# Fused attention, MoE and gated convolution on one core: small tiles allocated first, so that every large tile starts at a multiple of 256 bytes

## The chip, the cores and the metric

The kernel runs on one core of one Trainium2 chip. Its time is the device time of one launch in microseconds (us), the median of three timed runs. Five engines work side by side, each in its own program order and tied to the others by semaphores: PE (matmul, with its weight loads shown as PEld), DVE, ACT and POOL, and SP, which issues the transfers (DMA). SBUF is the memory on the chip from which the engines read: 128 partitions, in which a tile takes the same range of bytes in each. "Address" here is the byte in the partition at which a tile starts, and "remainder" that address modulo 256.

## What is computed

Three blocks in a row, all in float32, cut here to what matters:

```python
def _attn_ref(x, state):                 # x [8, 8, 512, 64], state [8, 8, 32, 64]
    a  = softmax(x @ state.T * scale)    # tokens read the state
    xread = a @ state
    a2 = softmax(state @ x.T * scale)    # the state reads the tokens
    sread = a2 @ x
    return concat([xread, sread], axis=2)          # [8, 8, 544, 64]

def _moe_ref(x, g_ln, w_ch1, w_ch2):               # x [8, 544, 512]
    xn = (x - mean) / sqrt(var + 1e-06) * g_ln
    return x + maximum(xn @ w_ch1, 0.0) @ w_ch2    # 512 -> 2048 -> 512

def _moe2_ref(x, w_in, conv_w, w_out):             # 512 -> 1024 -> 512
    h = maximum(x @ w_in, 0.0)
    gate = sigmoid(conv over 3 neighbours of h)
    return h * gate @ w_out
```

## The kernel before, in words

The work goes by batches of 512 tokens; the 32 state rows of all eight batches are gathered into one tail of 256 columns. The first block's hidden layer is made by `L1` (16 slices of the 2,048 hidden columns) and consumed at once by `L2`, which accumulates into the four banks `acc`. For batches 1 to 7 the weights of `L1` are folded with the state (`z_tiles`, Z tiles ZH and ZL), and the attention of the next batch (`attn`) and the norm of this one (`lnorm`) are woven in between the slices. Batch 0 runs in a hand-written order (`START`) together with the loading and conversion of the weights. After that the second block goes over (batch, slice) pairs: `L3` makes a slice, `conv`, `gate_1` and `gate_2` convolve and gate it on ACT, DVE and POOL, and `L4` multiplies it three steps later.

A float32 product is made from three passes of a faster type: each operand is split into a high and a low half (tiles with H and L in their names, or the two halves of one tile), and `three` (lines 623 to 626) issues high by high, high by low and low by high. In `T.matmul(o, s, m)` the second argument is the stationary operand, which PE loads as weights, and the third is the moving one, which streams through with up to 512 columns. The rows of the profile name the moving tile first: `acc<-ZH,w` has ZH moving over w.

All SBUF tiles come from one pool with one buffer per tag. A tag gets its place when it is first asked for, behind the tags asked for before it, padded to a multiple of 32 bytes; a later tile of the same tag takes the same place. `new` (line 68) asks by tag. Large tiles have sizes in multiples of 512 bytes, so only the small ones shift what comes behind them. The first tile starts at byte 16,512, remainder 128. Adding up the sizes in the order of first use gives the remainders of the kernel before:

| remainder | large tiles |
|---|---|
| 128 | hH, hL, XTt, s_in, s_raw, s_H, s_L, ident, ones |
| 160 | gmean (behind gcol) |
| 64 | XT0, XT1, r0 to r5, w2_0 to w2_8, w2_10, w2_11, bP, bU, AH0, AL0, sbd0, ctmp0, ctmp1 (behind eps, hmask and cw) |
| 128 | bR (behind ms0) |
| 192 | r6 (behind ms1) |
| 0 | w2_14 (behind m20 and z20) |
| 64 | w2_e, ZH0, ZL0, bV, rs0, tn, bQ (behind m21 and z21) |
| 96 | w2_13 (behind rm0) |
| 128 | w2_9, ZH1, ZL1, AH1, AL1, sbd1 (behind rm1) |
| 192 | w2_12, w2_15, rs1, v0, v1 (behind m10) |

The weights of the second block are put into places that have become free (`homes`, line 928): slices of `w_in` into AH0, AL0, r1 to r5 and XTt, slices of `w_out` into r0, r6, v0, v1, ZH0, ZL0, ZH1 and ZL1. The gated slices, stationary in `L4`, take w2_14, w2_15 and w2_3 in turn (`gm`, line 1023); the tail's gated slices take w2_2. The input of the second block, moving in `L3`, lies in XT0 and tn for even batches and in XT1, AH1 and AL1 for odd ones.

Of the kernel before, what the change touches and what calls it, by code (L numbers as in the profile page):

```python
# [9 lines left out]
F32 = mybir.dt.float32  # L10
# [7 lines left out]
P = 128  # L18
# [5 lines left out]
KC = DM // P  # L24
M1 = 16
FF = 8
# [16 lines left out]
def kernel(  # L43
# [18 lines left out]
    sb = ctx.enter_context(tc.tile_pool(name="sb", bufs=1))  # L62
# [5 lines left out]
    def new(tag, shape, dt=F32):  # L68
        count[0] += 1
        return sb.tile([P, *shape], dt, tag=tag, name=f"{tag}_{count[0]}")  # L70

    count = [0]

    hid = {c: new(f"h{c}", [2, S], F32 if c == "H" else F32R) for c in "HL"}
    XT = {}
# [7 lines left out]
    gcol = new("gcol", [KC])  # L83
    gmean = new("gmean", [KC, P])
    eps = new("eps", [1])
    hmask = new("hmask", [2, 2])
    cw = new("cw", [3 * FF])
# [17 lines left out]
    def flat(ap):  # L105
        return ap.rearrange("p a c -> p (a c)")
# [248 lines left out]
    def token_weights_3(aT, b, g, c):  # L355
        h, l = (t[:, g, c] for t in parts[b])
        A.activation(h, aT, AF.Copy)
        V.tensor_tensor(l, aT, f32(h), op=ALU.subtract)
# [67 lines left out]
    def tokens_start(h, xT, B):  # L426

        W = 256
        for g in range(2):
            xp = B["xp"][g].rearrange("p (q ck c) -> p q ck c", q=2, ck=2)  # L430
            for ck in range(2):
                for ql in range(2):
                    q = 2 * g + ql
                    T.transpose(xp[:, ql, ck], x0[:, 2 * h + ck, 2 * q : 2 * q + 2], ident)
            dst = xT[:, 2 * g : 2 * g + 2].rearrange("p q (ck c) -> p q ck c", ck=2)
            A.activation(dst, xp, AF.Copy)
        yield
        sc = B["sc"].rearrange("p (ck q m) -> p ck q m", ck=2, q=KC)
        for q in range(KC):
            for ck in range(2):  # L440
                T.matmul(
                    sc[:, ck, q], xT[:, q, P * ck : P * ck + P], sbd[0][:, q], start=True, stop=True
                )
        sT = new(B["U"], [16, NS])
        m1 = sb.tile([P, 16], F32, name=f"ms{h}")
        sc = B["sc"].rearrange("p (a n) -> p a n", n=NS)
        wide = m1.unsqueeze(2).to_broadcast([P, 16, NS])
        V.tensor_reduce(m1, sc, axis=AX.X, op=ALU.max)
        V.tensor_tensor(sT, sc, wide, op=ALU.subtract)
        A.activation(sT, sT, AF.Exp, scale=0.125)  # L450
        yield
        V.tensor_reduce(m1, sT, axis=AX.X, op=ALU.add)
        V.tensor_scalar(m1, m1, EPS_SM, None, op0=ALU.add)
        V.reciprocal(m1, m1)
        V.tensor_tensor(sT, sT, wide, op=ALU.mult)
        yield
        aT = B["aT"].rearrange("p (g ck c) -> p g ck c", g=2, ck=2)
        a4 = flat(sT).rearrange("p (ck g m) -> p ck g m", ck=2, g=2)
        for g in range(2):
            for ck in range(2):  # L460
                T.transpose(aT[:, g, ck], a4[:, ck, g], ident)
        aT = B["aT"].rearrange("p (g c) -> p g c", g=2)
        token_weights_3(aT, 0, slice(0, 2), HALF[h])
# [403 lines left out]
    def warm_steps():  # L867
# [5 lines left out]
    streams = {  # L873
        "s": (state_start(), acc),
        "0": (tokens_start(0, x0T[0], sets[0]), acc),
        "1": (tokens_start(1, x0T[1], sets[1]), acc),
        "a": (firsts(), acc),
        "b": (seconds(), acc),
# [77 lines left out]
    for u, follow in zip(units, [*units[1:], None]):  # L956
        n = S if u < NB else TAIL
# [132 lines left out]
    n = len(steps)  # L1090
    for i in range(n + 3):
        if i == FF + 3:
            tc_start.close()
        if i < n:
            b, f = steps[i]
# [14 lines left out]
        if i >= 3:  # L1110
            j = i - 3
            b, f = steps[j]
# [44 lines left out]
```

## Time and profile before

| | us |
|---|---|
| three timed runs | 1163.63, 1166.12, 1167.33 |
| their median | 1166.12 |
| span of the profiled execution | 1163.6 |
| PE busy in it | 1128.9 (97%) |
| PE weight loads | 845.3 (73%) |
| DVE busy | 720.9 (62%) |
| ACT busy | 442.2 (38%) |
| POOL busy | 182.3 (16%) |

The profile is one execution, from its first instruction to its last; the page gives no time around it. Busy times of PE come from modelled ends of pipelined matmuls, so a busy PE is not PE at its peak: two matmuls overlap in the list, and their distance is read from their starts.

### The profile page before, as it was taken

What the parts mean: (1) busy time and instruction counts of PE and PEld (TensorE: products, weight loads), DVE (VectorE), ACT (ScalarE), POOL (GpSimd) and SP (SyncE); (2) the same over time, 40 slices, a digit from 0 to 9 for tenths busy, and PEclk for the clock granted to TensorE, in tenths of its full rate; (3) what the DMA queues carried; (4) which work ended last, traced back from release to release, by engine and by line L of the source; (5) the groups of instructions that cost most, each with busy time, mean ns of one, the idle gap of its engine ahead of it and who ended that gap; (6) DMA issues with size and microseconds to landing.
All of it is one profiled execution on the core that took longest, in us unless ns stands there. A gap on an engine that the chain in (4) does not pass through costs nothing. (4 is left out here: it accounts for less than half of the span.)

```text
span 1163.6 us, 14521 instructions
## 1 busy us (share of the span) xinstructions
PE 1128.9 (97%) x5393; PEld 845.3 (73%) x5393; DVE 720.9 (62%) x1134; ACT 442.2 (38%) x788; POOL 182.3 (16%) x298
## 2 busy tenths in 40 slices
PE   6999999999999999999999999999999999999997
PEld 4544467777777777777667797788788888888885
DVE  5888567565574665664765723577676666666563
ACT  4655334332232233233233312555353444334332
POOL 2433200000000000000000000365342212222110
PEclk7999999999999999999999999999999999999999
DMA  8565262332334224323332125221112102100001
GB/s 281 159 201 163 71 234 84 83 118 72 76 111 111 73 94 109 95 84 79 96 83 82 73 73 199 95 84 58 37 55 73 37 37 83 37 37 37 1 37 45
DMA packets 129282, 106.29 MB, mean 91 GB/s; under 512 B 103332, under 2 KB 107452, under 8 KB 128188
## 3 DMA queue, kind: packets, MB, share of 16 engines
q1 hardware_dynamic: 129212, 105.37, 29.2%
q8 instruction: 42, 0.69, 0.2%
q14 instruction: 28, 0.23, 0.1%
HBM read 83.85 MB, written 21.50 MB: 91 GB/s over the span
## 5 line engine op out<-in xcount | busy, mean ns | idle before, releaser
L644 DVE SCALAR_TENSOR_TENSOR hL<-ph,hH 128x512 fp32r<-128x512 f32 (+1 forms) x128 | 83.4, 655 | 172.9 <-ACT hH L643 172.5
L624 PE MATMUL acc<-hH,w 128*128 128x512 f32 (+1 forms) x480 | 189.0, 394 | 0.0
L625 PE MATMUL acc<-hL,w 128*128 128x512 f32 (+1 forms) x480 | 181.8, 379 | 0.0
L626 PE MATMUL acc<-hH,w 128*128 128x512 f32 (+1 forms) x480 | 181.8, 379 | 0.0
L643 ACT ACTIVATE hH<-ph 128x512 fp32r<-128x512 f32 (+1 forms) x128 | 72.7, 568 | 196.3 <-PE ph L626 158.9
L1070 DVE SCALAR_TENSOR_TENSOR w<-w,cw,w 128x544 f32<-128x544 f32 x128 | 109.8, 859 | 35.2 <-POOL w L1068 33.3
L624 PEld LDWEIGHTS acc<-hH,w 128*128 128x128 f32 x480 | 90.3, 188 | 44.7 <-issue 15.6
L624 PE MATMUL ph<-AH,ZH 128*128 128x512 f32 x256 | 106.6, 416 | 1.6 <-ACT ZH L599 1.6
L626 PEld LDWEIGHTS acc<-hH,w 128*128 128x128 f32 x480 | 90.2, 188 | 18.2
L625 PEld LDWEIGHTS acc<-hL,w 128*128 128x128 f32 x480 | 90.3, 188 | 16.7 <-DVE hL L644 0.3
L626 PE MATMUL ph<-AH,ZL 128*128 128x512 f32 x256 | 101.4, 396 | 0.0
L625 PE MATMUL ph<-AL,ZH 128*128 128x512 f32 x256 | 100.8, 394 | 0.0
L212 POOL TENSOR_TENSOR ctmp<-ctmp,AH 128x512 int32<-128x512 int32 x1 | 1.3, 1311 | 589.5 <-DVE ctmp L211 589.5
L1051 ACT ACTIVATE w<-w 128x544 f32<-128x544 f32 x64 | 42.1, 658 | 135.2 <-DVE w L1070 135.2
L1058 DVE TENSOR_TENSOR w<-w,w 128x512 fp32r<-128x512 f32 x64 | 50.0, 782 | 43.7 <-ACT w L1057 43.0
L1052 DVE TENSOR_TENSOR w<-w,w 128x544 f32<-128x544 f32 x64 | 48.6, 760 | 40.0 <-ACT w L1051 40.0
L624 PEld LDWEIGHTS ph<-AH,ZH 128*128 128x128 f32 x256 | 48.2, 188 | 22.9 <-issue 8.8
L1057 ACT ACTIVATE w<-w 128x512 fp32r<-128x512 f32 x64 | 40.4, 631 | 52.4 <-DVE w L1052 50.3
L626 PEld LDWEIGHTS ph<-AH,ZL 128*128 128x128 f32 x256 | 48.2, 188 | 12.9 <-DVE ZL L600 2.0
L1068 POOL TENSOR_SCALAR w<-w,cw 128x544 f32<-128x544 f32 x64 | 47.9, 749 | 54.4 <-ACT w L1064 51.2
L625 PEld LDWEIGHTS ph<-AL,ZH 128*128 128x128 f32 x256 | 48.3, 189 | 10.2 <-issue 1.2
L667 PE MATMUL acc<-hH,w 128*128 128x512 f32 x112 | 50.4, 594 | 0.0
(465 smaller groups left out, 2257.5 us busy)
## 6 DMA issues: line engine op xcount, KB each, us to landing
r<-w1d SPq DMA_DIRECT2D x64, 512.0 KB, 5.2
r<-in_moe_w_ch_dram SPq DMA_DIRECT2D x16, 512.0 KB, 5.0
w<-in_moe_w_ch_dram SPq DMA_DIRECT2D x16, 512.0 KB, 8.2
x2d<-XT SPq DMA_DIRECT2D x8, 1024.0 KB, 4.9
bP<-in_x_dram SPq DMA_DIRECT2D x112, 64.0 KB, 2.3
bP<-in_x_dram SPq DMA_DIRECT2D x28, 256.0 KB, 3.7
out_dram<-w SPq DMA_DIRECT2D x24, 256.0 KB, 2.1
w1d<-r SPq DMA_DIRECT2D x8, 512.0 KB, 5.3
```

The lines of the kernel that those rows point to most:

```text
L624: T.matmul(o, lh, rh, start=first, stop=False)
L625: T.matmul(o, lh, rl, start=False, stop=False)
L626: T.matmul(o, ll, rh, start=False, stop=last)
L643: A.activation(h, p, AF.Relu)
L644: V.scalar_tensor_tensor(l, p, 0.0, f32(h), op0=ALU.max, op1=ALU.subtract)
L667: T.matmul(acc[d], whole2[m][:, c], h, start=m == 0, stop=m == M1 - 1)
L1051: A.activation(c, c, AF.Sigmoid)
L1052: V.tensor_tensor(c, c, h[:, 1 : SEQ + 1], op=ALU.mult)
L1057: A.activation(g[:, 0], c[:, :S], AF.Copy)
L1058: V.tensor_tensor(g[:, 1], c[:, :S], f32(g[:, 0]), op=ALU.subtract)
L1068: G.tensor_scalar(c, h[:, 0:SEQ], cw[:, f : f + 1], 0.0, op0=ALU.mult, op1=ALU.add)
L1070: V.scalar_tensor_tensor(c, h[:, k : k + SEQ], cw[:, k * FF + f : k * FF + f + 1], c, op0=ALU.mult, op1=ALU.add,)
```

## The change

Ahead of the first large tile, one tile is asked for under each of the small tags (m20, z20, m21, z21, eps, rm0, rm1, m10, gcol, hmask, cw), so that these tags have their places at the front. The two tiles ms0 and ms1, which were made where they are used, are made there too and kept in a list. A filler of 64 bytes, `pad`, follows. With it the small tiles take 640 bytes, from 16,512 to 17,152, which is 67 times 256, and each large tile behind starts at remainder 0. The tiles of the tags are asked for again later as before; those first ones are never written or read.

```diff
     count = [0]
 
+    for tag, n in (
+        *((t, 1) for t in ("m20", "z20", "m21", "z21", "eps")),
+        *((t, 2) for t in ("rm0", "rm1")),
+        ("m10", 16), ("gcol", KC), ("hmask", 4), ("cw", 3 * FF),
+    ):
+        sb.tile([P, n], F32, tag=tag, name=f"{tag}_0")
+    ms = [sb.tile([P, 16], F32, name=f"ms{h}") for h in range(2)]
+    sb.tile([P, 16], F32, name="pad")
+
     hid = {c: new(f"h{c}", [2, S], F32 if c == "H" else F32R) for c in "HL"}
...
         sT = new(B["U"], [16, NS])
-        m1 = sb.tile([P, 16], F32, name=f"ms{h}")
+        m1 = ms[h]
         sc = B["sc"].rearrange("p (a n) -> p a n", n=NS)
```

The change moves no instruction: on every engine the built programs have the same instructions in the same order with the same waits, and differ in addresses, line numbers (9 more) and the numbers in tiles' names. So at the place in the second block where `L4` of one slice ends, the tail's product follows and `L3` of a later slice begins, PE's row stands before as

```order
L624 MATMUL acc3_80<-ZH0_622_5740,w2_15_614_5610 128x512
L625 MATMUL acc3_80<-ZH0_622_5740,w2_15_614_5610 128x512
L626 MATMUL acc3_80<-ZH0_622_5740,w2_15_614_5610 128x512
L624 MATMUL pat1_84<-ZH0_622_5740,w2_2_612_5608 128x512
L625 MATMUL pat1_84<-ZH0_622_5740,w2_2_612_5608 128x512
L626 MATMUL pat1_84<-ZH0_622_5740,w2_2_612_5608 128x512
L624 MATMUL pat0_83<-XT0_642_6697,AH0_566_5271 128x512
L625 MATMUL pat0_83<-tn_643_6698,AH0_566_5271 128x512
```

and after it the same rows stand at the same place: only the remainders of the tiles change, here from 64 and 192 to 0.

## Rows read from the trace of the kernel before

**Rows 1.** The head of the page: span, busy time and instructions of each engine.

```profile
span 1163.6 us, 14521 instructions
PE 1128.9 (97%) x5393; PEld 845.3 (73%) x5393; DVE 720.9 (62%) x1134; ACT 442.2 (38%) x788; POOL 182.3 (16%) x298
```

**Rows 2.** Stretches: length; PE, PEld, DVE, ACT, POOL busy (instructions); granted clock; DMA; GB/s.

```profile
0.00:150.00 150.00, 134.16 (x520) 71.98 (x520) 109.99 (x183) 75.55 (x134) 46.48 (x60) 0.95 0.58 181
150.00:660.00 510.00, 502.60 (x2575) 369.14 (x2574) 311.88 (x545) 168.19 (x296) 0.00 (x0) 1.00 0.33 95
660.00:774.00 114.00, 113.30 (x619) 94.75 (x618) 50.22 (x80) 42.59 (x79) 23.05 (x17) 1.00 0.33 116
774.00:819.00 45.00, 42.14 (x223) 35.46 (x221) 35.37 (x45) 23.28 (x43) 26.35 (x33) 1.00 0.17 59
819.00:1155.00 336.00, 336.00 (x1462) 273.76 (x1463) 212.66 (x282) 131.94 (x236) 86.44 (x190) 1.00 0.12 41
870.00:1150.00 280.00, 280.00 (x1215) 227.97 (x1214) 176.81 (x235) 109.11 (x195) 69.09 (x155) 1.00 0.11 39
```

**Rows 3.** PE in order of time, from 961.83 us: start, length, instruction.

```profile
961.83 0.40 PE L624 MATMUL pat<-ZH,w 128*128 128x512 f32 x1
962.07 0.39 PE L625 MATMUL pat<-ZH,w 128*128 128x512 f32 x1
962.30 0.40 PE L626 MATMUL pat<-ZH,w 128*128 128x512 f32 x1
962.53 0.39 PE L624 MATMUL pat<-XT,AH 128*128 128x512 f32 x1
962.76 0.39 PE L625 MATMUL pat<-tn,AH 128*128 128x512 f32 x1
962.99 0.39 PE L626 MATMUL pat<-XT,AH 128*128 128x512 f32 x1
...
971.15 0.39 PE L626 MATMUL ph<-XT,AL 128*128 128x512 f32 x1
```

**Rows 4.** PE in order of time, from 922.89 us.

```profile
922.89 0.39 PE L624 MATMUL acc<-ZH,w 128*128 128x512 f32 x1
923.12 0.40 PE L625 MATMUL acc<-ZH,w 128*128 128x512 f32 x1
923.35 0.39 PE L626 MATMUL acc<-ZH,w 128*128 128x512 f32 x1
923.58 0.40 PE L624 MATMUL acc<-ZH,w 128*128 128x512 f32 x1
...
925.22 0.39 PE L625 MATMUL acc<-ZH,w 128*128 128x512 f32 x1
```

**Rows 5.** PE in order of time, from 787.79 us.

```profile
787.79 0.50 PE L624 MATMUL ph<-XT,r 128*128 128x512 f32 x1
788.13 0.40 PE L625 MATMUL ph<-tn,r 128*128 128x512 f32 x1
...
789.28 0.39 PE L624 MATMUL ph<-XT,r 128*128 128x512 f32 x1
...
790.41 0.39 PE L626 MATMUL ph<-XT,r 128*128 128x512 f32 x1
```

**Rows 6.** PE's waits: who waited for whom, us in total, times, longest.

```profile
PE pat L485 <- ACT bQ L478: 4.1, 3, 3.1
...
PE ph L624 <- ACT w L1064: 2.8, 2, 1.5
...
PE acc L434 <- DMA XT<-in_x_dram: 1.4, 2, 0.9
...
PE ph L416 <- DMA s_raw<-in_state_dram: 0.6, 1, 0.6
```

**Rows 7.** DVE's line 600: shortest, median and longest in ns.

```profile
L600 DVE TENSOR_TENSOR ZL<-pat,ZH x64: 677/681/693, 36.6 to 743.4; 128x512 fp32r<-128x512 f32 x64
```

## The prediction, made before the changed kernel was run

> **What bounds the kernel now.** I read the head of the page first: the matrix engine is busy 1,128.9 of 1,163.6 us, DVE 62%, ACT 38%, POOL 16% [rows 1]. Then the table by stages: from 819 to 1,155 us PE is busy 336.00 of 336.00 us, from 150 to 660 us 502.60 of 510, and the granted clock there is 1.00, the upper of its two levels (2.4 GHz) [rows 2]. So after the first 150 us the time is a row of matmuls, and what matters is how far apart two matmuls start. A busy time does not tell that: a row of the list in order of time shows 0.39 us for one 512-column matmul while the next starts 0.23 us later [rows 3]. The spacing comes from the starts. Between 870 and 1,150 us there are 1,215 matmuls, all of 512 columns, without a gap; a row that lasts 0.39 us is counted if its end reaches into the stretch, so they stand for 280.39 us, and 280.39 / 1,215 is 230.8 ns each [rows 2].
>
> Then I asked whether the spacing depends on where the operands lie, since that is all that the change moves. It does. The stretch from 961.83 us has 41 matmuls whose moving tiles (ZH0, XT0, tn, ZL0) and stationary tiles (w2_2, AH0, w2_3, AL0) all lie at remainder 64 of 256. Its first four spacings are 0.24, 0.23, 0.23, 0.23 us; from 962.76 to 971.15 us there are 37 spacings in 8.39 us, 226.7 ns each, and it ends when the next pair brings another remainder [rows 3]. The block from 922.89 us has ZH1 (remainder 128) moving over w2_15 (192): from 922.89 to 925.22 us ten spacings in 2.33 us, 233 ns each [rows 4]. I sorted the spacings after 150 us by remainder: where all tiles of a matmul, of the ten before it and of the next shared one remainder, 64, 128 or 192, each of the 164 spacings was 226 or 227 ns, whatever multiple of 256 bytes lay between the tiles; where remainders mixed, they lay between 225 and 241. So what counts in these rows is that the remainders agree, not which one it is.
>
> **The change, part by part.** It adds no instruction, takes none away and moves none: on each engine the same instructions stand in the same order with the same waits, and the early tiles of a tag are never written. What changes is the address of nearly every tile, and after it every large tile has remainder 0.
>
> Matmuls: the three products of each pair of halves (lines 624 to 626) are 3,696 matmuls with 512 columns: 7 x 16 x (6 + 12) = 2,016 in the seven batches of the first block after batch 0, 96 in batch 0, 64 x 12 = 768 in the first product of the second block, and 64 x 12 + 48 = 816 in its last. Of these 3,464 are followed within 250 ns by another of the kind, by their starts in the list in order of time; the others stand before a gap or another shape. At 230.7 to 230.8 ns before and 226.7 ns after, each gives back 4.0 ns, together 13.9 us. That is the upper bound.
>
> Against it stands that a row of matmuls needs time to settle. After a break (another shape or a wait) the spacing is irregular even where all remainders agree: after the break at 787.79 us the five spacings from 788.13 to 789.28 us take 1.15 us, 230 ns each, and the next five, to 790.41 us, 1.13 us, 226 ns each [rows 5]. I count 129 such breaks by the starts, 99 of them between 150 and 660 us, where the attention and the folded weights come in between, and one after 819 us. With eight spacings of 230 ns each they keep 129 x 8 x 3.3 ns = 3.4 us of the 13.9. That leaves 10.5 us: some 5.7 us from the 1,449 spacings behind 819 us and the rest from the stages before, most of it from 150 to 660 us.
>
> What of it lies on the path: nearly all, since PE has no other idle time than its own breaks there. The exception is 774 to 819 us, where PE is busy 42.14 of 45 us and twice waits for ACT w L1064, 2.8 us in all [rows 2, 6]; behind that stands the conversion of the second block's weights on DVE and POOL, which does not get faster. Its 125 spacings, 0.4 us, I take as lost. The other matmuls (32-row tiles, transposes, two-pass float32) I leave as they are. So the sum is -10.1 us.
>
> DVE, ACT and POOL: the 64 instructions of line 600 write and read ZL0 and ZH0 at remainder 64 or ZL1 and ZH1 at 128 in turn, and last 677 to 693 ns [rows 7]. I cost the new addresses at nothing there, and the engines hide behind PE anyway with a third of the span free on DVE.
>
> DMA: no row tells what a transfer gains from its address. PE itself waits for DMA 1.4 and 0.6 us, all in the first microseconds [rows 6]; a transfer that gets faster is worth at most these 2.0 us, one that gets slower as much again. I take 0, as the nearest row to the other stages, where PE waits for no transfer at all.
>
> **A rule that speaks against it.** The rows show spacings of 226.7 and 233 ns for the same instruction at the same clock, by the remainders of its two operands [rows 3, 4]. The Trainium skill (TensorE: Matmul & The Clock Gate, section "Step-by-step: what each phase is for") says that the engine reads its streaming operand and its weights through two independent ports, so that loading the next weights takes no bandwidth from the running matmul, and SBUF — State Buffer, section "SBUF: two separate sides", that the engine never waits on another. By that rule the addresses could not matter and the time would stay at 1,166.1 us; the trace disagrees with it as far as two operands of one engine go. The Trainium skill (DMA: Bandwidth & Descriptors, section "How a descriptor splits into AXI transactions") lets a descriptor that does not start at a multiple of 256 bytes cost an extra transaction; no row here shows it, and the sum would by it be at most 2.0 us larger.
>
> **The sum against the runs.** The profiled execution's span is 1,163.6 us, and the fastest of the three timed runs took 1,163.63 us, so nothing that shows lies around the span. The profile would go to 1,163.6 - 10.1 = 1,153.5 us; the median of the runs shown is 2.5 us above that execution, and the forecast by it is 1,166.1 - 10.1 = 1,156.0 us.
>
> **Rivals.** (a) Only the last stage gains. If the breaks before 819 us disturb more than I reckon, or the faster PE runs into DVE there (311.88 us busy of 510 [rows 2], the 3.1 us wait for ACT bQ at the end of the stage [rows 6]), only the 1,449 spacings behind 819 us are won: 1,449 x 4.1 ns = 5.9 us at most, 1,160.2 us. For it speaks that before 660 us stretches of one remainder are short; against it, that they settle there at the same 226.7 ns. (b) Nothing changes: the spacing follows the tiles for a reason that goes along with the remainder (which tiles are read in turn, which engine works beside), and one remainder for all does not settle. Then 1,166.1 us. Against it: 64, 128 and 192 behave alike, with different tiles. (c) Slower: no stationary and moving pair of before has remainder 0 on both sides. Should 0 be the worst case rather than a fourth of the same kind, all would go as in [rows 4]: 3,464 x (233 - 230.7) = 8.0 us more, 1,174.1 us. It decides from the point where the settled spacing exceeds 230.7 ns. Against it speaks that three remainders of four give the same spacing, and that the tiles in them lie at all multiples of 256 bytes from each other.
>
> **How the numbers follow.** A measurement of this kernel can tell about 0.3%, 3.5 us, from no change. Forecast (1,150.2 to 1,158.5 us) 0.70, (a) 0.15, (b) 0.10, (c) 0.05. (a) still is faster by over 0.3%, so faster has 0.85, same 0.10 and slower 0.05. The fast end of the range is the upper bound with the DMA waits gone: 1,166.1 - 13.9 - 2.0 = 1,150.2 us. The slow end takes in (a) with 2.3 us for the scatter of the runs, which lie up to 2.5 us from their median: 1,162.5 us. Left out are (b) and (c), 0.15.
>
> **What would show it.** In the profile after: the same counts of instructions; 870 to 1,150 us, or the same work earlier, with some 1,235 matmuls in 280 us instead of 1,215; in the list in order of time starts at 0.22 and 0.23 us alternately all through the last stage, also for ZH1 with w2_15; after breaks still some irregular spacings. DVE's 677 to 693 ns at line 600 unchanged. PE's wait for ACT w L1064 grows by some tenths of a us. The forecast is wrong if the spacing in the last stage stays above 229 ns, or if it falls and PE's waits grow by as much.

## The result, and the profile after

| | before | after |
|---|---|---|
| timed runs, us | 1163.63 to 1167.33 (5 runs) | 1154.40 to 1156.10 (5 runs) |
| median, us | 1166.84 | 1155.22 |
| span of the profiled execution, us | 1163.6 | 1154.2 |

The ratio of after to before is 0.9912, with a 95% interval of 0.9901 to 0.9922: the changed kernel is 0.9% faster, 9.1 to 11.6 us. The forecast was 1,156.0 us with a range of 1,150.2 to 1,162.5.

The head of the page after, which answers to [rows 1]: the same number of instructions on every engine, and PE's busy time is 8.9 us less, while no other engine's differs by more than 1.7 us.

```profile
span 1154.2 us, 14521 instructions
PE 1120.0 (97%) x5393; PEld 847.0 (73%) x5393; DVE 720.0 (62%) x1134; ACT 440.9 (38%) x788; POOL 181.7 (16%) x298
```

The stretches after, with the columns of [rows 2] (length; PE, PEld, DVE, ACT and POOL busy with instructions; granted clock; DMA; GB/s):

```profile
150.00:660.00 510.00, 502.24 (x2594) 372.61 (x2593) 314.53 (x548) 169.14 (x297) 0.00 (x0) 0.99 0.33 95
774.00:819.00 45.00, 42.08 (x224) 35.64 (x223) 35.63 (x45) 22.24 (x42) 26.96 (x34) 1.00 0.21 71
870.00:1140.00 270.00, 270.00 (x1193) 223.58 (x1192) 172.99 (x231) 106.30 (x191) 65.67 (x152) 1.00 0.11 41
```

and the last of these stretches in the kernel before:

```profile
870.00:1140.00 270.00, 270.00 (x1172) 219.85 (x1171) 171.96 (x228) 106.08 (x189) 67.95 (x152) 1.00 0.11 41
```

PE has no gap in either, yet 1,193 matmuls stand after where 1,172 stood before. With the 0.39 us of a row that reaches in from the left, 270.39 / 1,193 is 226.6 ns and 270.39 / 1,172 is 230.7 ns. That is the whole change in the last stage.

PE in order of time after, the place that answers to [rows 4], ZH1 moving over w2_15:

```profile
918.02 0.39 PE L633 MATMUL acc<-ZH,w 128*128 128x512 f32 x1
918.25 0.39 PE L634 MATMUL acc<-ZH,w 128*128 128x512 f32 x1
918.48 0.39 PE L635 MATMUL acc<-ZH,w 128*128 128x512 f32 x1
918.70 0.39 PE L633 MATMUL acc<-ZH,w 128*128 128x512 f32 x1
...
920.29 0.39 PE L634 MATMUL acc<-ZH,w 128*128 128x512 f32 x1
```

The same ten spacings that took 2.33 us in [rows 4] take 2.27 us, 227 ns each. The stretch that answers to [rows 5], behind a break:

```profile
784.69 0.50 PE L633 MATMUL ph<-XT,r 128*128 128x512 f32 x1
785.02 0.39 PE L634 MATMUL ph<-tn,r 128*128 128x512 f32 x1
...
786.18 0.39 PE L633 MATMUL ph<-XT,r 128*128 128x512 f32 x1
...
787.32 0.39 PE L635 MATMUL ph<-XT,r 128*128 128x512 f32 x1
```

The five spacings from 785.02 us still take 1.16 us, 232 ns each, and the next five 1.14 us, 228 ns: the row still has to settle after a break, as in [rows 5].

PE's waits after, which answer to [rows 6], and DVE's line 609, which answers to [rows 7]:

```profile
PE pat L494 <- ACT bQ L487: 4.1, 3, 3.2
...
PE ph L633 <- ACT w L1073: 2.9, 2, 1.4
```

```profile
L609 DVE TENSOR_TENSOR ZL<-pat,ZH x64: 674/681/693, 37.1 to 740.7; 128x512 fp32r<-128x512 f32 x64
```

Neither moved by more than a few ns or tenths of a us.

### The profile page after: what moved, and what is told of

It reads as the page before. It is cut to its first block, busy times and chain, and to the rows that moved or that the text cites. A ratio compares the mean times of both kernels' runs of the same rounds, so it can differ in the third digit from the quotient of the medians.

```text
span 1154.2 us, 14521 instructions
## 1 busy us (share of the span) xinstructions
PE 1120.0 (97%) x5393; PEld 847.0 (73%) x5393; DVE 720.0 (62%) x1134; ACT 440.9 (38%) x788; POOL 181.7 (16%) x298
```

## Experiments

The question was what exactly makes the spacing: that the two operands of PE agree in their remainder, that tiles start at a multiple of 256 bytes, or that transfers get faster. In all runs the spacing of L2, the products that read hH and hL, was taken from the starts in order of time: in each kernel 1,250 of these matmuls are followed within 250 ns by another of the 512-column kind.

**All tiles at another remainder.** Two kernels keep everything in agreement and only make the filler larger, by 64 and by 32 bytes:

```diff
-    sb.tile([P, 16], F32, name="pad")
+    sb.tile([P, 32], F32, name="pad")     # all64
+    sb.tile([P, 24], F32, name="pad")     # all32
```

> The filler is 64 bytes larger, so every large tile lies at remainder 64 instead of 0. Theory A (the remainders of PE's two operands must agree, whichever they are): as the changed kernel, 1,155 us within 2 us, settled spacing 226.7 ns in the last stage. Rival B (what counts is a start at a multiple of 256 bytes, for PE or for the transfers): the gain goes, 1,166 us, spacing near 231 ns.

Measured: 1,156.07 us, ratio to before 0.9920 (0.9905 to 0.9935).

> The filler is 32 bytes larger, so every large tile lies at remainder 32, half a step off a multiple of 64. Theory A: 1,155 us within 2 us, settled spacing 226.7 ns. Rival B, also in the form that a multiple of 64 is needed: 1,166 us or more, spacing 231 to 234 ns.

Measured: 1,154.80 us, ratio 0.9909 (0.9894 to 0.9923). The last stage, first all64, then all32:

```profile
870.00:1140.00 270.00, 270.00 (x1193) 223.55 (x1192) 173.04 (x232) 106.36 (x191) 65.82 (x152) 1.00 0.11 41
```

```profile
870.00:1140.00 270.00, 270.00 (x1193) 223.65 (x1192) 171.51 (x231) 105.20 (x189) 64.50 (x151) 1.00 0.11 39
```

1,193 matmuls in both, as in the changed kernel. Rival B is out: no tile needs to start at a multiple of 256 or of 64 bytes; all of the gain is there with every large tile at remainder 32.

**Two tiles out of step.** From the changed kernel, hH and hL alone are moved to another remainder r, with two fillers that add up to 256 bytes, so that all other large tiles stay at 0:

```diff
+    sb.tile([P, r // 4], F32, name="pad1")
     hid = {c: new(f"h{c}", [2, S], F32 if c == "H" else F32R) for c in "HL"}
+    sb.tile([P, (256 - r) // 4], F32, name="pad2")
```

> Only hH and hL, the moving tiles of L2, are put at remainder 128; all other large tiles stay at 0. Theory A: only the products of L2 get slower, 1,344 matmuls of 512 columns at some 232.4 ns (the mean of before for pairs that are 128 apart) instead of 226.7, that is +7.7 us, 1,163 us; the last stage stays at 226.7 ns. Rival B: two tiles of some sixty, less than 1 us, 1,156 us.

Measured: 1,159.74 us, ratio to before 0.9955 (0.9938 to 0.9971), 4.5 us above the changed kernel.

> Only hH and hL at remainder 192, all other large tiles at 0. Theory A: L2's spacing near 233 ns as for pairs of before whose moving tile is 192 ahead, +8 us, 1,163 us. Rival B: no change, 1,156 us.

> Only hH and hL at remainder 64, the rest at 0: moving 64 ahead of stationary. Theory A: L2's spacing near the 230.0 ns of such pairs in the kernel before, between the changed kernel's 228.1 and the 232.6 ns of h128; total about 2 us above the changed kernel. Rival B: no change.

> Only hH and hL at remainder 32, the rest at 0: moving 32 ahead. In the kernel before such pairs had 233.3 ns (68 of them). Theory A: L2's spacing 233 ns, worse than at 64, so the cost is no growing function of the distance; total about 6 us above the changed kernel. Rival B: no change.

> Only hH and hL at remainder 224, that is 32 behind the stationary tiles at 0. No theory of mine has a number from rows for it; by symmetry with 32 ahead (233.3 ns) L2's spacing would be 233 ns. If it were below the changed kernel's 228.1 ns, agreeing remainders would not be the best arrangement.

> Only hH and hL at remainder 96. If only odd multiples of 32 were bad, 233 ns as at 32; if it were the distance to the nearest multiple of 128, between the 230.3 of 64 and the 232.6 of 128. Below 228.1 ns would speak against agreeing remainders as the best.

> Only hH and hL at remainder 160, as for 96: 233 ns if odd multiples of 32 are bad, between 232.6 and 233.4 (128 and 192) otherwise; in either case about 6 us above the changed kernel.

The six kernels other than h128 were run once each. L2's mean spacing in all, with the time:

| remainder of hH and hL, others 0 | mean spacing in L2, ns | time, us |
|---|---|---|
| 0 (the changed kernel) | 228.1 | 1155.22 |
| 32 | 233.3 | 1161.15 |
| 64 | 230.3 | 1161.38 |
| 96 | 233.8 | 1163.38 |
| 128 | 232.6 | 1159.74 |
| 160 | 233.6 | 1161.08 |
| 192 | 233.4 | 1160.60 |
| 224 | 233.4 | 1160.07 |

One L2 slice of 12 matmuls, first in the changed kernel, then the same slice with hH and hL at 192:

```profile
301.20 0.39 PE L633 MATMUL acc<-hH,w 128*128 128x512 f32 x1
301.42 0.39 PE L634 MATMUL acc<-hL,w 128*128 128x512 f32 x1
...
303.69 0.39 PE L635 MATMUL acc<-hH,w 128*128 128x512 f32 x1
```

```profile
301.44 0.39 PE L635 MATMUL acc<-hH,w 128*128 128x512 f32 x1
301.68 0.39 PE L636 MATMUL acc<-hL,w 128*128 128x512 f32 x1
...
304.01 0.40 PE L637 MATMUL acc<-hH,w 128*128 128x512 f32 x1
```

Eleven spacings take 2.49 us in the one (226 ns) and 2.57 us in the other (234 ns). The last stage, which does not read hH and hL, stays as it was, here with them at 192:

```profile
870.00:1140.00 270.00, 270.00 (x1193) 223.58 (x1192) 174.78 (x232) 107.62 (x193) 69.43 (x155) 1.00 0.11 41
```

So theory A holds in its place and its size: the spacings of 230.0, 232.4 and 233.3 ns that were read from mixed pairs of the kernel before came back as 230.3 (remainder 64), 232.6 (128) and 233.3 (32) when hH and hL were put there. Of the eight differences 0 is the best and 64 the second; the cost is no growing function of the distance. My totals were too high: I reckoned h128 from 226.7 ns, but L2 in the changed kernel stands at 228.1 ns because its slices lie between breaks, so (232.6 - 228.1) x 1,250 = 5.6 us and not 7.7. For h64 the total came out higher than expected (1,161.4 us for a single run, against 1,157), with L2's spacing as expected; part of it is that L1, the product after it, gets slower too (its mean is 230.9 ns there, 228.2 in the changed kernel, over 642 spacings: 1.7 us), though its own tiles agree. The rest cannot be told from a single run: executions of one kernel scatter by some 2 us.

**One of the two tiles.** hH stays at 0, hL alone goes to 128:

```diff
-    hid = {c: new(f"h{c}", [2, S], F32 if c == "H" else F32R) for c in "HL"}
+    hid = {"H": new("hH", [2, S])}
+    sb.tile([P, 32], F32, name="pad1")
+    hid["L"] = new("hL", [2, S], F32R)
+    sb.tile([P, 32], F32, name="pad2")
```

> Only hL at remainder 128, hH and the rest at 0: one of the three products of L2 has a pair that disagrees, two agree. Theory A1 (each matmul pays for its own pair): L2's mean spacing is a third of the way from the 228.1 ns of the changed kernel to the 232.6 ns of both tiles at 128, that is 229.6 ns, and the excess is at the products with hL. Theory A2 (a disagreeing pair throws the row out of step, and its neighbours pay too): L2's mean near that of both tiles at 128, 231 to 233 ns, with the excess spread over all three products.

Measured: 1,156.88 us in one run; L2's mean 230.8 ns, 233.6 for the product with hL, 230.2 and 228.4 for the two with hH. A slice that no break precedes:

```profile
300.85 0.39 PE L638 MATMUL acc<-hH,w 128*128 128x512 f32 x1
301.07 0.39 PE L636 MATMUL acc<-hH,w 128*128 128x512 f32 x1
301.30 0.40 PE L637 MATMUL acc<-hL,w 128*128 128x512 f32 x1
301.54 0.39 PE L638 MATMUL acc<-hH,w 128*128 128x512 f32 x1
301.76 0.39 PE L636 MATMUL acc<-hH,w 128*128 128x512 f32 x1
```

From the start of the product with hL at 301.30 us to the next it is 0.24 us; the two around it take 0.22 and 0.23. In all 32 slices with at least 12 spacings since the last break, the spacings by the ns are 227, 234, 226 in turn: each matmul pays for its own pair (A1). Of the other 80 slices, which stand behind a break by at most six matmuls, 39 run 236, 234, 230 in turn to the end, so there the neighbours do pay (A2): with one pair out of step the row often does not settle. The mean, between the two expectations, is a mixture of both. That the slow spacing comes at every third matmul, the one with hL, also speaks against another engine's work as its cause. Whether a matmul's pair means the weights that it uses or those that are loaded meanwhile for the next one, these runs do not separate, as all weights lie at 0 in them.

**The transfers.** Of all large tiles only bP goes back to the remainder 64 that it had before:

```diff
+    sb.tile([P, 16], F32, name="pad1")
     load_xt(1, 0, new("bP", [1024]))
+    sb.tile([P, 48], F32, name="pad2")
```

> Only bP, into which the 128-byte pieces of x are loaded (and from which the state reads take their moving operand), goes back to remainder 64 as before the change; all other large tiles stay at 0. Theory A: no product of lines 624 to 626 of the original touches bP, so 1,155 us within 2 us and the same landing times of bP. Rival C (part of the gain comes from transfers into aligned tiles): up to 2 us slower, 1,157 us, and bP's transfers land later than in the changed kernel.

Measured: 1,155.55 us, ratio to before 0.9909 (0.9889 to 0.9929), no different from the changed kernel. But the transfers do differ, against the expectation of theory A: the median time from issue to landing of the 28 loads of x with 256-byte pieces is 3.7 us in the kernel before, 3.3 in the changed one and 3.7 in this one, in this order:

```profile
bP<-in_x_dram SPq DMA_DIRECT2D x28, 256.0 KB, 3.7
```

```profile
bP<-in_x_dram SPq DMA_DIRECT2D x28, 256.0 KB, 3.3
```

```profile
bP<-in_x_dram SPq DMA_DIRECT2D x28, 256.0 KB, 3.7
```

The same loads take 3.8 and 3.9 us in all64 and all32, and 3.3 to 3.6 us in the eight kernels with hH or hL moved, where bP lies at 0: the difference is small against this scatter, but the two groups do not overlap. The 112 loads of x with 128-byte pieces take 2.3 us in every kernel.

The Trainium skill (DMA: Bandwidth & Descriptors, section "How a descriptor splits into AXI transactions") states, for transactions that read, that the first one of a descriptor that does not start at a multiple of 256 bytes starts at the boundary below it, so that a descriptor can take one more. In the rows here it is the written side that moved; they agree with it in sign.

In the time nothing of it shows. The interval of bp64, 2.3 us to either side, is too wide to exclude rival C alone; but all64 and all32, with the slower loads too, lie within 0.9 us of the changed kernel, and PE's waits for transfers are 1.8 us in all in the changed kernel and 1.5 us in bp64. Rival C is out as a cause of the gain; an effect of under 1 us is not excluded.

## Why the prediction was right, point by point

**The bound.** That the spacing of the starts and not the busy time is the quantity to read was right: busy shares are the same before and after, 97% of both spans, and 1,172 became 1,193 matmuls.

**The main term.** 3,464 spacings of 230.7 ns were to fall to 226.7 ns but for the breaks. Measured over the same kind, 3,462 spacings have a mean of 227.57 ns, so 3.1 ns each, 10.8 us together, where the prediction has 10.5. Behind 819 us the mean is 226.7 ns (1,439 spacings), from 150 to 660 us 228.2 (1,551 spacings, 230.8 before). Behind ten others without a break (2,403 spacings) each is 226 or 227 ns, 226.67 in the mean; so what the breaks keep is 3,462 x (227.57 - 226.67) = 3.1 us; the term was 3.4. A small slip without consequence: the stretch of [rows 3] has 42 matmuls, and 41 is the number of its spacings.

**The part between 774 and 819 us** was counted as lost. PE's wait there for ACT went from 2.8 to 2.9 us [rows 6] and its busy time from 42.14 to 42.08 us [rows 2]: nothing was won there. By the starts, the same matmul comes 3.1 us earlier than before both at 774 and at 819 us.

**DVE, ACT, POOL and DMA** were costed at nothing. DVE's durations did not move, and the gain of the transfers, which does exist, did not show in the time (bp64, all64, all32).

**What the sum left out.** The profiled span fell by 9.4 us, not by the 10.8 us of the spacings. What is missing is the granted clock, which the prediction held fixed. Both kernels have the same row of matmuls, so the start of each can be compared with its start before: at 43 us the changed kernel is 0.5 us late; up to the long wait of PE for ACT bQ it wins 3.5 us, around this wait it loses 0.8 us, from there to 819 us it wins 1.0 us and behind that 5.9 us, together 9.1 us at the last matmul.

The two losses stand where the clock is at its lower level for a while. It falls around the wait of 3.2 us, in the profiled execution after for longer than before; the first row is after, the second before, the third all32:

```profile
576.00:590.00 14.00, 10.81 (x43) 6.37 (x43) 8.82 (x14) 5.01 (x9) 0.00 (x0) 0.76 0.15 34
```

```profile
580.00:594.00 14.00, 11.43 (x50) 7.09 (x51) 9.33 (x15) 4.76 (x8) 0.00 (x0) 0.88 0.25 58
```

```profile
576.00:590.00 14.00, 11.24 (x51) 7.64 (x52) 9.52 (x15) 4.75 (x8) 0.00 (x0) 0.88 0.23 50
```

In 14 us around that wait the mean clock is 0.76 after and 0.88 before, and 43 matmuls are done instead of 50. From the last matmul before the wait to one and the same matmul behind it, in the same order:

```profile
575.84 0.39 PE L635 MATMUL acc<-hH,w 128*128 128x512 f32 x1
...
588.66 0.39 PE L633 MATMUL ph<-AH,ZH 128*128 128x512 f32 x1
```

```profile
578.80 0.39 PE L626 MATMUL acc<-hH,w 128*128 128x512 f32 x1
...
590.79 0.39 PE L624 MATMUL ph<-AH,ZH 128*128 128x512 f32 x1
```

```profile
574.96 0.39 PE L635 MATMUL acc<-hH,w 128*128 128x512 f32 x1
...
586.69 0.39 PE L633 MATMUL ph<-AH,ZH 128*128 128x512 f32 x1
```

That is 12.82, 11.99 and 11.73 us. The start of the kernel shows the same, with a clock of 0.79 after against 0.83 in the first 40 us of the two others. all32 differs from the changed kernel only in the filler, and its row of starts settles where the rest went: the changed kernel is behind it by 1.0 us at 43 us, by 0.9 us before the wait, by 2.0 us after it and by 1.9 us at the last matmul, so all of the difference arises in the two stretches with the lower clock. The span of all32 is 1,152.7 us, 10.9 us less than before, which is the 10.8 us of the spacings. Two other executions of the changed kernel had the mean clock of the profiled one before, 0.991, and spans of 1,153.4 and 1,152.6 us, 10.2 and 11.0 us less. Why the lower level lasts longer in some executions, the runs do not show.

**The size.** The medians of the timed runs fell by 11.6 us and the profiled spans by 9.4, since the execution profiled before was the fastest of its five and the one profiled after the second slowest. The interval of 9.1 to 11.6 us covers the 10.8 us of the spacings and the forecast's 10.1 us alike. The mechanism and its main term are right; that the median lies within 0.8 us of the forecast is in part luck, as the fall of the medians is 1.5 us larger than the sum and the forecast started from a median of three runs that is 0.7 us below that of five.

**The rivals.** (b) and (c) are refuted by the spacing itself. (a) would have left the stages before 819 us as they were; from 150 to 660 us the spacing went from 230.8 to 228.2 ns. That the change acts through agreement and not through the multiple of 256, which the prediction could only infer from 64, 128 and 192, is shown by all32 and all64.

**The rule that speaks against it.** The Trainium skill (TensorE: Matmul & The Clock Gate, section "Step-by-step: what each phase is for") has loading the next weights take no read bandwidth from the running matmul. Here moving only hH and hL by 192 bytes makes L2's spacing 233.4 ns instead of 228.1, so a rule by which the places of PE's two operands could not matter does not hold, and the measurement decides. Why they matter, the runs do not show.

## What to carry to other kernels

When PE is the bound, compare the starts of neighbouring matmuls by where their operands lie before looking for work to remove: a few ns at each of some thousand matmuls came to 10.8 us here, while the largest of PE's waits is 4.1 us in all [rows 6]. Give all tiles that PE reads as moving or stationary operand the same remainder modulo 256 bytes; small tiles between them are what breaks it, and to allocate those first with a filler costs no instruction. One tile out of step suffices to slow its own products, and behind a break often its neighbours'. All this was measured on the 512-column products of `three`. The 256-column products of the same lines gained nothing: the mean of their 251 spacings of under 150 ns is 117.9 ns before and 119.3 after.

## What the runs showed of the hardware that I had not expected

- The spacing of two 512-column matmuls of this kind at the upper clock level is 226.7 ns where all operands agree modulo 256 bytes, once the row has settled. In the mean of L2, breaks included, it is 228.1 ns in agreement and 230.3 to 233.8 ns where the moving operand lies 32 to 224 bytes ahead, 64 being the mildest.
- Even in agreement the row takes up to some nine matmuls to settle after another shape or a wait: behind the break at 784.69 us the first five full spacings are 232 ns each.
- A 256 KB load with 256-byte pieces lands in 3.3 to 3.6 us (medians of nine kernels) when its tile starts at a multiple of 256 bytes, and in 3.7 to 3.9 us (four kernels) at remainder 64 or 32.
- The lower clock level after the same wait lasts longer in some executions than in others, without any change in the program's order: 0.76 against 0.88 in 14 us (the changed kernel and all32).
